# A spectral filter and a two-layer product in one kernel: where the halves of the second product, the splits of the weights and the first load of w_out stand

## The chip, the cores and the metric

The kernel runs on one core of a Trainium2 chip. The metric is the time on the device in microseconds (us). In what follows PE is the matrix engine (TensorE), PEld its weight loads, DVE is VectorE, ACT is ScalarE, POOL is GpSimd and SP is SyncE, which here only issues DMAs.

## The reference

Two parts follow each other. A spectral filter works along the sequence of 3008 positions, for 8 batches of 256 features, and its result goes through two matrix products with a leaky ReLU between them.

```python
X = np.fft.rfft(x, axis=1)                       # x: (8, 3008, 256)
Yr = Xr @ w_r - Xi @ w_i + b_r                   # w_r, w_i: (256, 256)
Yi = Xr @ w_i + Xi @ w_r + b_i
Yr, Yi = soft_threshold(Yr, 0.01), soft_threshold(Yi, 0.01)
y = np.fft.irfft(Yr + 1j * Yi, n=3008, axis=1)   # then reshaped to (24064, 256)
h = y @ w_in                                     # w_in: (256, 2048), as 64-bit floats
g = np.maximum(0.01 * h, h)
out = g @ w_out                                  # w_out: (2048, 256), as 64-bit floats
```

## The kernel before

**The spectral part.** 3008 is 47 x 64, so each Fourier transform is done as two smaller ones by matrix products, per batch `b`. `fwd(b)` makes the transform of length 47 (lines 219 to 322) and stores it in DRAM as `u_dram`. `mid(b)` (lines 325 to 461) reads it back in twelve pieces as tiles `u`, makes the transform of length 64 (`stage_b`, line 358), splits the result into a high and a low part, the tiles `eh` and `el` (lines 366 to 375), applies w_r and w_i (`proj`), thresholds (lines 405 to 407, tile `t`, in the list `thresholded`), multiplies by signs (lines 411 and 415), splits into `zh` and `zl` (lines 420 to 424), transforms back (`stage_g`) and stores `v_dram`. `inverse` makes the last transform from tiles `vin` read back from `v_dram`. For batch 0 `fwd` and `mid` run ahead of everything else, in plain 32-bit matmuls; they are the start. For the batches 1 to 7 they are generators that are woven into the two products, and they use high and low parts of the weights, which `split_consts` makes (lines 108 to 113: one ACT copy at line 112 and one DVE subtraction at line 113 for each of six tiles).

**The two products.** Every number is a high and a low part, and each product of two blocks is three matmuls: high by high, high by low, low by high. Tokens come in 47 chunks of 512, `ci`; the 2048 middle columns in eight pieces, `q`. This gives 376 steps. In a step the first product is done by seven block products instead of eight (a Strassen-Winograd scheme). `moe_a` (line 549) makes four of them, in two PSUM banks `b1` and `b2` of 2 x 256 columns: 12 matmuls at line 92. ACT then copies one quarter to `p1` (line 559), and DVE adds: `u2` (line 560), and the fourth quarter of the tile `g`, which the profile calls `gf` (lines 562 and 563). `moe_b` (line 566) adds the other three block products to the same banks: 9 matmuls at line 92. They overwrite what lines 559 to 563 read, so they wait for them. Then come ACT at line 573, DVE at line 574, ACT at line 576 (the leaky ReLU), ACT's copy `gh` (line 578, high part) and DVE's subtraction `gl` (line 580, low part). `moe_o` (line 583) makes the second product of a step in two halves, `eh` 0 and 1, of 6 matmuls of 512 columns each, at line 593. It runs `LAG` = 2 steps behind, so it reads `gh` and `gl` of two steps ago.

**What sets the order.** On each engine the instructions run in a fixed order. A scheduler sorts them when the program is built, by a simulated timeline of its own. `in_order` (line 84) binds the matmuls of `moe_a`, `moe_b` and `moe_o` to each other in the order in which `moe` (line 624) issues them; the other instructions the scheduler places around them. `tc.issue_after(x)` keeps an instruction behind `x` in that order.

**The loads of w_out.** `load_wout` (line 175) reads it in eight pieces of 512 KB into tiles `raw`. The first two take the buffers of `gl`, which are free in the start.

Of the kernel before, what the change touches and what calls it, by code (L numbers as in the profile page):

```python
# [18 lines left out]
N1, N2, NK1 = 47, 64, 24  # L19
# [11 lines left out]
def spectral_mlp_kernel(  # L31
# [35 lines left out]
    sync, act, dve, pool = nc.sync, nc.scalar, nc.vector, nc.gpsimd  # L67
# [16 lines left out]
    def in_order(part, *args):  # L84

        with tc.issue_after(mlp[0].ins) if mlp else nullcontext():
            part(*args)
# [87 lines left out]
    def load_wout():  # L175

        n = CS // D
        ov = w_out.bitcast(U32).rearrange("(a p) f -> p a f", p=P)
        raws = []

        def load(early):
            k = len(raws)
            tag, bufs = ("gl", 2) if early else (("e", 1), ("z", 1))[k % 2]
            raw = sb.tile([P, CS, 2], U32, name="raw", tag=tag, bufs=bufs)
            with tc.issue_after(zeroed[0].ins):
                pool.dma_start(raw.rearrange("p (a f) w -> p a (f w)", a=n), ov[:, k * n:(k + 1) * n, :])
            raws.append(raw)

        for k in range(2):
            load(True)  # L190
        yield 1
        consts["wout"] = tuple(
            sb.tile([P, NF, D], F32R, name=f"wout_{p}", tag=f"wout_{p}", bufs=1) for p in ("hi", "lo"))
        for c in range(NF // n):
            a = sb.tile([P, CS], F32, name="cva", tag="zf", bufs=1)
            q = sb.tile([P, CS], F32, name="cvq", tag="u", bufs=3)
            float64_parts(raws[c], a, q)
            dh, dl = (w[:, c * n:(c + 1) * n, :] for w in consts["wout"])
            a, q = (t.rearrange("p (a f) -> p a f", a=n) for t in (a, q))
            act.copy(dh, a)  # L200
            dve.tensor_sub(a, a, dh.bitcast(F32))
            converted.append(dve.tensor_add(dl, a, q))
            yield 1
            while c >= 1 and len(raws) < min(c + 3, NF // n):
                load(False)
# [2 lines left out]
    u_dram = {}  # L208
    v_dram = {}

    reads, written, turned, turning, thresholded, zeroed = [], [], [], [], [], []
    NX = -(-NS // 2)

    XW = [(0, 2), (2, 6), (6, 10), (10, 13)]
# [110 lines left out]
    def mid(b):  # L325
# [51 lines left out]
        def proj(j):  # L377

            e = e_t.pop(j)
            ps_k = bank("psf", 2) if b else bank("pso", 2)  # L380
            ps_y = None if b else bank("psf", 2)

            for dst, c, w in ((0, 2, "wr"), (0, 1, "wn"), (D, 0, "wd")):
                if c == 1 and b:
                    ps_y = bank("psf", 2)
                products((ps_k if c == 2 else ps_y)[:, dst:dst + D], [
                    (tuple(t[:, a, c, :] for t in e), tuple(t[:, a, :] for t in consts[w]) if b else (consts[w + "32"][0][:, a, :],)) for a in range(NH)
                ] + ([((ones,), (bz[:, D if c == 0 else 0:][:, :D],))] if b == 0 and c < 2 else []))
                if c == 2:
                    kc = sb.tile([P, D], F32, name="kc", tag="kc")  # L390
                    act.copy(kc, ps_k[:, :D])  # L391
                if c == 2 and b:
                    kb = sb.tile([P, 2, D], F32, name="kb", tag="kb", bufs=1)
                    pool.tensor_add(kb, bias, kc.unsqueeze(1).broadcast_to([P, 2, D]))  # L394
                if c:
                    yield 6 * D
                if c == 2 and b and j:
                    stage_g(j - 1)
                    yield 3 * CS
            t = sb.tile([P, 2, D], F32, name="t", tag="t" if b else "v", bufs=1 if b else 2)  # L400
            c = sb.tile([P, 2, D], F32, name="c", tag="kb", bufs=1)
            if b == 0:
                dve.tensor_add(t, ps_y.rearrange("p (r d) -> p r d", r=2), kc.unsqueeze(1).broadcast_to([P, 2, D]))
            else:
                dve.tensor_add(flat(t), ps_y, flat(kb))
            dve.tensor_scalar(c, t, LAMBDA, -LAMBDA, ALU.min, ALU.max)
            thresholded.append(dve.tensor_sub(t, t, c))
            zf = z0[j % 3] if b == 0 else sb.tile([P, 2, D], F32, name="zf", tag="zf", bufs=1)
            for i in range(2):
                s = slice(64 * i, 64 * (i + 1))  # L410
                act.copy(zf[:64, i, :], t[s, 0, :])  # L411
                if b == 0 and j == NPAIR - 1:
                    dve.tensor_scalar(zf[64:, i, :], t[s, 1, :], sign[s, NK1 + j:NK1 + j + 1], None, ALU.mult)
                else:
                    act.mul(zf[64:, i, :], t[s, 1, :], sign[s, NK1 + j:NK1 + j + 1])  # L415
            if b == 0:
                z_t[j] = (zf,)
                yield 6 * D
                return
            z = sb.tile([P, 2, 2, D], F32R, name="zh", tag="z", bufs=1)  # L420
            zh, zl = z[:, 0], z[:, 1]
            act.copy(zh, zf)
            dve.tensor_sub(zl, zf, zh.bitcast(F32))
            z_t[j] = (zh, zl)
            yield 6 * D
# [198 lines left out]
    def moe():  # L624

        for i, (ci, q) in enumerate(steps):
            if q == 0:
                nxt = tokens(ci + 1) if ci + 1 < nch else iter(())
            in_order(moe_a, ci, q)
            if i >= LAG:  # L630
                in_order(moe_o, *steps[i - LAG], 0)
            next(nxt, None)
            yield ci + (q + 0.5) / NQ
            in_order(moe_b, ci, q)
            if i >= LAG:
                in_order(moe_o, *steps[i - LAG], 1)
            next(nxt, None)
            if q == NQ - 1:
                for _ in nxt:
                    pass  # L640
            yield ci + (q + 1) / NQ
        for s in steps[-LAG:]:
            for eh in range(NH):
                in_order(moe_o, *s, eh)
# [34 lines left out]
    sign = const.tile([P, NK1 + NPAIR], F32, name="sign")  # L679
# [14 lines left out]
    with tc.issue_after(turned[0].ins):  # L694
        act.copy(bz[:1], brow[:1])
        act.copy(bz[32:33], brow[32:33])
        act.mul(fa32[:, 2], fa32[:, 1], -1.0)
        split_consts()
    dve.tensor_sub(bz[32:33], brow[32:33], bz[32:33].bitcast(F32))
    m0 = Stream(mid(0), MID)  # L700
    m0.to(0.001)
# [12 lines left out]
    for i in range(1, 17):  # L714
        m0.to(i / 16)
        if i in (1, 5, 8):
            load_win(1 + i // 4, (sync, sync), reads[-1])
        if i in (5, 10):
            convert_win(i // 5)
        if 5 <= i < 12:  # L720
            next(fp.gen)
        if i == 13:
            next(wout)
        if i >= 14:

            if i < 16:
                next(fp.gen)
# [144 lines left out]
```

## Time and profile before

| | |
|---|---|
| median of 3 runs | 2892.94 us (2890.22 to 2896.18) |
| profiled execution | 2892.13 us, its span 2890.3 us |
| busy share of the span | PE 93%, PEld 80%, DVE 65%, ACT 58%, POOL 9% |
| mean granted clock of PE | 0.985 |

The start ends at about 130 us, when the first matmul of the products runs. From there to about 2400 us the products run beside the spectral part of the other batches, and then nearly alone. Rows of a timeline read: start, duration, engine, line, operation, what it writes and reads, and in brackets how long the engine was idle before it and what ended that. Rows of waits read: who waited for whom, us in total, how often, the longest. A matmul's listed duration is longer than the distance to the next one, since matmuls overlap; distances between starts tell what PE gets done.

### The profile page before, as it was taken

Reading aid. Unit: us, or ns where it says so; the run is one execution under the profiler, and the core shown is the slowest. Engines: PE = TensorE matmul, PEld = TensorE weight load, DVE = VectorE, ACT = ScalarE, POOL = GpSimd, SP = SyncE. Lnnn points to the kernel's source line nnn. Section 1 sums busy time; section 2 is a strip of 40 time slices with the busy share of each in tenths; the row PEclk is TensorE's granted clock in tenths of the full one; section 3 lists DMA queues with packets and bytes.
Section 4 is the critical chain, followed back from the end, with each engine's and each line's share of the span. In section 5 each row is a group of like instructions: output and inputs, shape, how many; then the busy total and the mean of one; then the engine's idle time right before and its main releaser. Section 6 shows DMA issues by size and latency. Waiting matters only on the chain.

```text
span 2890.3 us, 43048 instructions
## 1 busy us (share of the span) xinstructions
PE 2673.7 (93%) x16300; PEld 2307.6 (80%) x16300; DVE 1892.0 (65%) x3403; ACT 1671.0 (58%) x3174; POOL 248.9 (9%) x188
## 2 busy tenths in 40 slices
PE   6799999999999999999999999999999999999988
PEld 4578878888788887888878887788887888777777
DVE  5787766666666666676666666666666766555554
ACT  4667655656566654666546565566555665454443
POOL 0001120001200011000110001100011000000000
PEclk9999999999999999999999999999999999999999
DMA  9422132111321112121221112211122111000000
GB/s 253 141 79 55 44 94 59 42 48 30 98 63 46 37 50 76 55 58 33 62 79 51 42 35 61 82 57 40 33 67 81 55 44 33 25 25 15 15 8 15
DMA packets 117416, 165.16 MB, mean 57 GB/s; under 512 B 13437, under 2 KB 69401, under 8 KB 117209
## 3 DMA queue, kind: packets, MB, share of 16 engines
q1 hardware_dynamic: 79473, 115.02, 13.1%
q10 hardware_dynamic: 36584, 43.20, 5.9%
q0 software_dynamic: 1152, 4.19, 0.5%
q8 instruction: 128, 2.10, 0.3%
q14 instruction: 79, 0.65, 0.1%
HBM read 86.60 MB, written 75.76 MB: 56 GB/s over the span
## 4 chain that ended last, share of the span: by engine, by line
PE 46%; DVE 27%; ACT 18%; issue 4%; DMA 3%; POOL 1%; SPq 0%; DVEq 0%; ACTq 0%; POOLq 0%
PE psh L92 18%; PE pso L593 16%; PE psf L78 7%; DVE gl L580 7%; ACT gh L578 6%; ACT gf L576 5%; DVE gf L574 4%; DVE gf L562 3%; DVE u L560 2%; DVE gf L563 2%; PE psf L496 2%; PE psf L358 2%; ACT zf L415 2%; DVE yl L523 1%; ACT zf L411 1%
## 5 line engine op out<-in xcount | busy, mean ns | idle before, releaser
L92 PE MATMUL psh<-yh,win_hi 128*128 128x256 f32 x2632 | 791.7, 301 | 113.9 <-DVE gf L563 78.3
L580 DVE TENSOR_TENSOR gl<-gf,gh 128x1024 fp32r<-128x1024 f32 x376 | 465.2, 1237 | 441.6 <-ACT gh L578 434.2
L92 PE MATMUL psh<-yl,win_hi 128*128 128x256 f32 x2632 | 741.1, 282 | 0.0
L92 PE MATMUL psh<-yh,win_lo 128*128 128x256 f32 x2632 | 739.4, 281 | 0.0
L92 PEld LDWEIGHTS psh<-yh,win_hi 128*128 128x128 f32 x2632 | 499.5, 190 | 235.1 <-DVE gf L563 122.9
L593 PE MATMUL pso<-gh,wout_hi 128*128 128x512 f32 x1504 | 597.4, 397 | 0.0
L593 PE MATMUL pso<-gh,wout_lo 128*128 128x512 f32 x1504 | 597.1, 397 | 0.0
L593 PE MATMUL pso<-gl,wout_hi 128*128 128x512 f32 x1504 | 594.5, 395 | 0.0
L576 ACT ACTIVATE gf<-gf 128x768 f32<-128x768 f32 x376 | 318.2, 846 | 437.0 <-DVE gf L574 427.1
L92 PEld LDWEIGHTS psh<-yl,win_hi 128*128 128x128 f32 x2632 | 500.4, 190 | 23.6 <-issue 0.6
L92 PEld LDWEIGHTS psh<-yh,win_lo 128*128 128x128 f32 x2632 | 499.3, 190 | 0.3 <-issue 0.2
L578 ACT CAST gh<-gf 128x1024 fp32r<-128x1024 f32 x376 | 395.1, 1051 | 10.3 <-PE pso L593 4.0
L574 DVE TENSOR_TENSOR gf<-psh,u 128x512 f32<-128x512 f32 x376 | 258.4, 687 | 199.7 <-PE psh L92 199.2
L593 PEld LDWEIGHTS pso<-gl,wout_hi 128*128 128x128 f32 x1504 | 285.9, 190 | 65.4
L593 PEld LDWEIGHTS pso<-gh,wout_hi 128*128 128x128 f32 x1504 | 286.0, 190 | 35.0
L593 PEld LDWEIGHTS pso<-gh,wout_lo 128*128 128x128 f32 x1504 | 286.0, 190 | 31.8
L573 ACT ACTIVATE gf<-psh 128x256 f32<-128x256 f32 x376 | 145.3, 386 | 258.6 <-PE psh L92 238.8
L394 POOL TENSOR_TENSOR kb<-bias,kc 128x512 f32<-128x512 f32 x84 | 127.1, 1513 | 1616.0 <-ACT kc L391 1507.9
L560 DVE TENSOR_TENSOR u<-psh,p 128x256 f32<-128x256 f32 x376 | 157.1, 418 | 90.5 <-ACT p L559 90.4
L562 DVE TENSOR_TENSOR gf<-psh,u 128x256 f32<-128x256 f32 x376 | 158.7, 422 | 28.2
L563 DVE TENSOR_TENSOR gf<-psh,gf 128x256 f32<-128x256 f32 x376 | 157.8, 420 | 6.1
L559 ACT COPY p<-psh 128x256 f32<-128x256 f32 x376 | 137.2, 365 | 14.9 <-PE psh L92 13.0
(135 smaller groups left out, 3271.8 us busy)
## 6 DMA issues: line engine op xcount, KB each, us to landing
u<-u_dram SPq DMA_DIRECT2D x192, 128.0 KB, 2.7
out_dram<-ob SPq DMA_DIRECT2D x94, 256.0 KB, 2.0
vin<-v_dram SPq DMA_DIRECT2D x96, 240.0 KB, 3.3
v_dram<-v ACTq DMA_DIRECT2D x168, 128.0 KB, 2.4
xin<-x_dram SPq DMA_DIRECT2D x85, 240.0 KB, 3.0
u_dram<-xin ACTq DMA_DIRECT2D x72, 240.0 KB, 2.4
raw<-w_out_dram POOLq DMA_DIRECT2D x8, 512.0 KB, 5.0
win_raw<-w_in_dram SPq DMA_DIRECT2D x8, 512.0 KB, 7.6
```

The costliest lines, as they stand in the source:

```text
L78: last = nc.tensor.matmul(dst, a, b, start=(i == 0), stop=(i == len(terms) - 1))
L92: mlp[:] = [nc.tensor.matmul(dst, a, b, start=start and i == 0, stop=i == 2, skip_group_check=True)]
L559: act.copy(p1, b1[:, lo])
L560: dve.tensor_add(u2, b1[:, hi], p1)
L562: dve.tensor_add(g[:, 3], b2[:, hi], u2)
L563: dve.tensor_add(g[:, 3], b2[:, lo], g[:, 3])
L573: act.activation(g[:, 0], b1[:, lo], AF.Prelu, alpha=SLOPE)
L574: dve.tensor_add(g[:, 1:3], b2.rearrange("p (k n) -> p k n", k=2), u2.unsqueeze(1).broadcast_to([P, 2, HT]))
L576: act.activation(g[:, 1:4], g[:, 1:4], AF.Prelu, alpha=SLOPE)
L578: cp = act.copy(gh, g)
L580: parted[:] = [cp, dve.tensor_sub(gl, g, gh.bitcast(F32))]
L593: mlp[:] = [nc.tensor.matmul(po, a[:, f, s], r[:, i], start=(f == 0 and j == 0), stop=(f == NF - 1 and j == 2),)]
```

## The change

Four things change.

In `moe`, both halves of the second product now stand between `moe_a` and `moe_b`. Before, the second half stood behind `moe_b`.

`split_consts` is called in turn 4 of the loop over `mid(0)`, behind the latest threshold and the latest sign multiplication issued by then, which a new list `signed` records. Before, it was called ahead of `mid(0)`.

The first two loads of w_out are issued by SP, behind the last load of `u` for batch 0 (`reads[-1]`). Before, POOL issued them behind its first memset.

The later loads of w_out stay on POOL as they were.

```diff
-            with tc.issue_after(zeroed[0].ins):
-                pool.dma_start(raw.rearrange("p (a f) w -> p a (f w)", a=n), ov[:, k * n:(k + 1) * n, :])
+            with tc.issue_after(reads[-1].ins if early else zeroed[0].ins):
+                (sync if early else pool).dma_start(raw.rearrange("p (a f) w -> p a (f w)", a=n), ov[:, k * n:(k + 1) * n, :])
...
-                    act.mul(zf[64:, i, :], t[s, 1, :], sign[s, NK1 + j:NK1 + j + 1])
+                    signed[:] = [act.mul(zf[64:, i, :], t[s, 1, :], sign[s, NK1 + j:NK1 + j + 1])]
...
             yield ci + (q + 0.5) / NQ
-            in_order(moe_b, ci, q)
             if i >= LAG:
                 in_order(moe_o, *steps[i - LAG], 1)
+            in_order(moe_b, ci, q)
...
         act.mul(fa32[:, 2], fa32[:, 1], -1.0)
-        split_consts()
...
+        if i == 4:
+            with tc.issue_after(thresholded[-1].ins), tc.issue_after(signed[-1].ins):
+                split_consts()
```

How this moves instructions is shown at three places. First PE, at one step of the last stage. `psh` are the banks `b1` and `b2`, `pso` the sums of the second product, one for each half; the numbers tell tiles apart. Before:

```order
L593 MATMUL pso_27365<-gl_27571,wout_hi_886 128x512
L92 MATMUL psh_27628<-yh_27027,win_hi_169 128x256
L92 MATMUL psh_27628<-yl_27028,win_hi_169 128x256
L92 MATMUL psh_27628<-yh_27027,win_lo_170 128x256
L92 MATMUL psh_27629<-yh_27027,win_hi_169 128x256
L92 MATMUL psh_27629<-yl_27028,win_hi_169 128x256
L92 MATMUL psh_27629<-yh_27027,win_lo_170 128x256
L92 MATMUL psh_27629<-yh_27027,win_hi_169 128x256
L92 MATMUL psh_27629<-yl_27028,win_hi_169 128x256
L92 MATMUL psh_27629<-yh_27027,win_lo_170 128x256
L593 MATMUL pso_27388<-gh_27569,wout_hi_886 128x512
```

And PE at the same step of the changed kernel:

```order
L593 MATMUL pso_27365<-gl_27577,wout_hi_886 128x512
L593 MATMUL pso_27372<-gh_27575,wout_hi_886 128x512
L593 MATMUL pso_27372<-gh_27575,wout_lo_887 128x512
L593 MATMUL pso_27372<-gl_27577,wout_hi_886 128x512
L593 MATMUL pso_27372<-gh_27575,wout_hi_886 128x512
L593 MATMUL pso_27372<-gh_27575,wout_lo_887 128x512
L593 MATMUL pso_27372<-gl_27577,wout_hi_886 128x512
L92 MATMUL psh_27628<-yh_27027,win_hi_169 128x256
```

The nine matmuls of `moe_b` stood between the halves; now the second half (`pso_27372`) follows the first, and `moe_b` follows it.

Second DVE, in the same stage. Before, from line 574 of one step to that of the next:

```order
L574 TENSOR_TENSOR gf_25211<-psh_25194,u2_25208 128x512
L580 TENSOR_TENSOR gl_25246<-gf_25211,gh_25244 128x1024
L560 TENSOR_TENSOR u2_25275<-psh_25260,p1_25274 128x256
L562 TENSOR_TENSOR gf_25278<-psh_25261,u2_25275 128x256
L563 TENSOR_TENSOR gf_25278<-psh_25261,gf_25278 128x256
L574 TENSOR_TENSOR gf_25278<-psh_25261,u2_25275 128x512
```

And DVE between the same two instructions of the changed kernel:

```order
L574 TENSOR_TENSOR gf_25211<-psh_25194,u2_25208 128x512
L560 TENSOR_TENSOR u2_25275<-psh_25260,p1_25274 128x256
L562 TENSOR_TENSOR gf_25278<-psh_25261,u2_25275 128x256
L563 TENSOR_TENSOR gf_25278<-psh_25261,gf_25278 128x256
L580 TENSOR_TENSOR gl_25252<-gf_25211,gh_25250 128x1024
L574 TENSOR_TENSOR gf_25278<-psh_25261,u2_25275 128x512
```

The subtraction `gl` of a step stood ahead of the next step's lines 560 to 563, and now stands behind them. On ACT, in the same way, line 559 of the next step has moved from behind lines 576 and 578 to ahead of them.

Third PE, in the middle of the program, at a projection of batch 2: line 358 transforms a tile `u`, and line 78 with `wr` and `eh` is the first matmul that reads what is made of the result. Before:

```order
L358 MATMUL psf_4449<-fb_94,u_4174 128x2x64 x4
L92 MATMUL psh_4323<-yh_3794,win_hi_169 128x256
L92 MATMUL psh_4323<-yl_3795,win_hi_169 128x256
L92 MATMUL psh_4323<-yh_3794,win_lo_170 128x256
L78 MATMUL psf_4488<-wr_hi_177,eh_4454 128x256
```

And PE in front of the same projection (`eh_4454`) in the changed kernel; its transform stands 43 rows ahead of it:

```order
L593 MATMUL pso_4276<-gh_4610,wout_hi_886 128x512
L593 MATMUL pso_4276<-gh_4610,wout_lo_887 128x512
L593 MATMUL pso_4276<-gl_4612,wout_hi_886 128x512
L593 MATMUL pso_4276<-gh_4610,wout_hi_886 128x512
L593 MATMUL pso_4276<-gh_4610,wout_lo_887 128x512
L593 MATMUL pso_4276<-gl_4612,wout_hi_886 128x512
L78 MATMUL psf_4488<-wr_hi_339,eh_4454 128x256
```

A whole second product and a `moe_a` now stand between the transform and the projection, where three matmuls did.

More of the change, by code (lines that the diff above doesn't have):

```diff
@@ L209, in spectral_mlp_kernel @@
     v_dram = {}
-    reads, written, turned, turning, thresholded, zeroed = [], [], [], [], [], []
+    reads, written, turned, turning, thresholded, zeroed, signed = [], [], [], [], [], [], []
     NX = -(-NS // 2)
```

## The prediction

> **What bounds the kernel now.** I read the page's busy shares first, then the three stages as windows, then who TensorE (PE) waited for in each stage, then one period of the last stage in order of time.
>
> ```profile
> PE 2673.7 (93%) x16300; PEld 2307.6 (80%) x16300; DVE 1892.0 (65%) x3403; ACT 1671.0 (58%) x3174; POOL 248.9 (9%) x188
> ...
> L92 PE MATMUL psh<-yh,win_hi 128*128 128x256 f32 x2632 | 791.7, 301 | 113.9 <-DVE gf L563 78.3
> L580 DVE TENSOR_TENSOR gl<-gf,gh 128x1024 fp32r<-128x1024 f32 x376 | 465.2, 1237 | 441.6 <-ACT gh L578 434.2
> ```
>
> PE is the bound: 93% busy, and most of its idle time stands before line 92, the seven block products of the first matrix product, waiting for a VectorE (DVE) addition. The next two views, the windows and the waits of PE alone, give start (0 to 200 us), middle (spectral work beside the two products, 200 to 2400) and end (the products nearly alone).
>
> ```profile
> 0.00:200.00 200.00, 152.97 (x703) 113.43 (x704) 140.78 (x258) 119.23 (x228) 8.04 (x15) 0.91 0.58 166
> 200.00:2400.00 2200.00, 2075.85 (x13009) 1824.00 (x13008) 1481.29 (x2673) 1318.16 (x2540) 239.55 (x172) 0.99 0.20 56
> 2400.00:2890.30 490.30, 444.90 (x2592) 370.21 (x2590) 269.96 (x474) 233.62 (x407) 1.29 (x1) 0.99 0.06 19
> ```
>
> Columns: length, busy time of PE, weight loads, DVE, ACT, POOL, then granted clock. In the end stage DVE works 55% and ACT 48% of the time, and PE still idles 45 us: a latency, not a throughput. Waits of PE, first the middle stage, then the end:
>
> ```profile
> PE psh L92 <- DVE gf L563: 46.1, 92, 2.0
> PE psh L92 <- DVE u L560: 20.4, 61, 1.1
> PE psf L78 <- ACT eh L373: 16.2, 9, 2.8
> PE psf L78 <- DVE xz L266: 11.6, 24, 1.8
> PE psf L78 <- DVE xz L267: 6.0, 16, 0.5
> PE psf L78 <- ACT zh L422: 5.0, 6, 2.0
> PE psf L78 <- DVE yc L529: 4.1, 2, 2.1
> ```
> ```profile
> PE psh L92 <- DVE gf L563: 26.6, 64, 1.7
> PE psh L92 <- DVE u L560: 10.4, 55, 0.5
> ```
>
> One period of the end stage:
>
> ```profile
> 2702.30 0.38 PE L92 MATMUL psh<-yh,win_hi 128*128 128x256 f32 x1 [0.17 <-DVE u L560]
> ...
> 2702.64 0.28 PE L92 MATMUL psh<-yh,win_lo 128*128 128x256 f32 x1
> 2702.81 0.42 DVE L563 TENSOR_TENSOR gf<-psh,gf 128x256 f32<-128x256 f32 x1
> ...
> 2703.29 0.39 PE L92 MATMUL psh<-yh,win_hi 128*128 128x256 f32 x1 [0.37 <-DVE gf L563]
> 2703.51 0.28 PE L92 MATMUL psh<-yl,win_hi 128*128 128x256 f32 x1
> ...
> 2704.10 0.40 PE L593 MATMUL pso<-gh,wout_hi 128*128 128x512 f32 x1
> 2704.30 0.69 DVE L574 TENSOR_TENSOR gf<-psh,u 128x512 f32<-128x512 f32 x1 [1.07 <-PE psh L92]
> ...
> 2705.03 0.85 ACT L576 ACTIVATE gf<-gf 128x768 f32<-128x768 f32 x1 [1.69 <-DVE gf L574]
> ...
> 2705.49 0.28 PE L92 MATMUL psh<-yh,win_hi 128*128 128x256 f32 x1
> ...
> 2705.91 1.05 ACT L578 CAST gh<-gf 128x1024 fp32r<-128x1024 f32 x1
> ...
> 2706.89 0.40 PE L593 MATMUL pso<-gh,wout_hi 128*128 128x512 f32 x1
> 2706.99 1.23 DVE L580 TENSOR_TENSOR gl<-gf,gh 128x1024 fp32r<-128x1024 f32 x1 [1.99 <-ACT gh L578]
> ...
> 2708.13 0.42 DVE L560 TENSOR_TENSOR u<-psh,p 128x256 f32<-128x256 f32 x1
> ...
> 2708.60 0.39 PE L92 MATMUL psh<-yh,win_hi 128*128 128x256 f32 x1 [0.17 <-DVE u L560]
> ```
>
> The reader is to see a loop. `moe_b` of a step ends at 2704.10; then L574 (0.69), L576 (0.85), L578 (1.05) and `gl` L580 (1.23) run one behind the other, and only behind `gl` does DVE come to L560, L562 and L563 of the next step, for which that step's `moe_b` waits. The period is 2708.60 - 2702.30 = 6.30 us. PE's own work in it: 12 matmuls of `moe_a` from 2705.49 to 2706.89, 1.40; two halves of six matmuls, each 2705.49 - 2704.10 = 1.39; nine matmuls of `moe_b` at 1.40/12 = 0.117, 1.05; in all 5.23. So 1.07 us a step is lost.
>
> **The change, part by part.** *Both halves of `moe_o` ahead of `moe_b`.* Between `moe_a`'s end and `moe_b`'s start PE now has 2.78 us of work instead of 1.39. The order shows that DVE and ACT were re-sorted too: L560, L562, L563 of a step now stand ahead of the `gl` before it. From `moe_b`'s end to the next `moe_b`'s second product PE has 1.40 + 2.78 + 0.35 = 4.53 us; the DVE chain there is 0.69 + 3 x 0.42 = 1.95 us plus passing times. 2.5 us of room is more than all waits seen in the end stage, so there I let them vanish. What a wait costs: at a spacing of 0.117 the matmul of 2703.29 would have stood at 2702.76, so it lost 0.53 where 0.37 is listed, and its successor came 0.22 behind it instead of 0.117: 0.26 on top of the listed idle time. End stage: 26.6 + 10.4 + 119 x 0.26 = 68 us. The ceiling is every step of the stage at 1.07:
>
> ```profile
> L560 DVE TENSOR_TENSOR u<-psh,p x73: 415/417/426, 2404.0 to 2877.1; 128x256 f32<-128x256 f32 x73
> ```
>
> 73 x 1.07 = 78 us. I take 68.
>
> Middle stage, the same two waits: 46.1 + 20.4 + 153 x 0.26 = 106 us. Here DVE also serves the spectral streams. It is busy 1481 us, of which some 295 steps take 1.24 + 0.69 + 3 x 0.42 = 3.19 us each, 941; the rest is 540, 1.8 us a step, against 2.5 us of room. On average it fits, but it comes in lumps, and all of a lump can stand ahead of L563. I take four fifths, 85 us; the ends are half (53) and all (106).
>
> What the wider lead costs: `gl` of a step is read by `moe_o` two steps later, and that lead shrinks by one half, 1.39 us: from 3 x 1.39 + 2 x 1.40 + 1.05 + two matmuls, 0.46 = 8.5 us to 7.1. The chain L574 to `gl` takes 0.69 + 0.85 + 1.05 + 1.23 = 3.8 us, a little over 4 with the passing times. Cost nothing; cover 3 us. `gh` and `gl` have two buffers, and are now free before they are rewritten, since their readers moved ahead.
>
> *The spectral streams, re-sorted by it.* In the middle a projection could stand right behind its input:
>
> ```profile
> 473.93 0.39 PE L78 MATMUL psf<-wr_hi,eh 128*128 128x256 f32 x1 [2.48 <-ACT eh L373]
> ```
>
> Before it stood only three matmuls behind the transform that feeds it (13 of 84 projections stand like that in the order); now the nearest has 18 rows between. So the waits for eh go: 16.2, with yc (which stands at the same place) 4.1, and 11 x 0.26, together 23 us. xz and zh, 22.6 + 46 x 0.26 = 35 us, are also spaced wider but keep short chains: half, 17 us. Sum 40; ends 10 (places change, waits stay) and 58.
>
> *The clock.* It was 0.99 in both stages, 1% of 2690 us, some 27 us lost, and as long waits go I give back 16; the ends are 0 and 27. [...]
>
> *Weights split in the middle stage of the start; w_out's first words by SP.* Before, ACT held six splits ahead of the first transform, and POOL sent 1 MB of w_out into the writes of u_dram:
>
> ```profile
> 37.74 0.62 ACT L112 CAST wn_hi<-w 128x512 fp32r<-128x512 f32 x1
> ...
> 38.38 3.60 PE L358 MATMUL psh<-fb,u 128*128 128x128 f32 x16 [14.82 <-ACT wn_hi L112]
> ```
> ```profile
> 108.03 0.70 ACT L131 ACTIVATE cvq<-raw 128x512 f32<-128x512 uint32 x1 [2.53 <-DMA raw<-w_out_dram]
> ```
> ```profile
> 0.00:50.00 50.00, 24.98 (x90) 16.32 (x91) 18.31 (x34) 17.41 (x32) 2.09 (x7) 0.86 0.88 252
> 50.00:100.00 50.00, 48.15 (x231) 37.27 (x230) 43.61 (x76) 44.38 (x87) 0.30 (x1) 1.00 0.73 200
> ```
>
> 1 MB at the 252 GB/s of the first 50 us (last column) is 4.2 us; this the first transform can gain if the u loads are what it waits for, nothing if not. Against it: the six splits, three at 0.62 and three of at most half that, 2.8 us of ACT and about as much of DVE, now fall where ACT is busy 44.4 of 50 us and PE 48.2, and the two w_out loads come late on SP, behind the last u loads, two issues that the stores of v behind them on SP wait for. If they land after ACT reaches them, ACT's queue stands as it did at 108.03, 2.53 us each. [...] From -4.2 to +2.8 + 5.1 = +7.9; I take 0, since the two sides are alike. POOL's queue only gets shorter.
>
> *The end.* Behind the last `moe_b` PE had 18 matmuls to cover the last chain, now 12: 1.39 us less, +1 us.
>
> Sum: 68 + 85 + 40 + 16 - 0 - 1 = 208. The profiled execution took 2892.1 us (span 2890.3 and 1.8 around it), 0.8 below the median of 2892.9. 2892.1 - 208 = 2684 us. A change under 0.2%, about 6 us, could not be told from none.
>
> **The rivals.** *The waits move inside the middle stage.* For it: DVE and ACT are fixed queues, and a shorter PE time raises their load from 67% to about 72% (1481 of 2200 - 141); against it, the room worked out above. Then the middle gives half, 53, the streams 10, the clock 5, the end stage still 68, less 1: 135, so 2757 us.
> *All of it goes.* 78 + 106 + 58 + 27 = 269, the start 4, less 1: 2620 us. Against it speak the lumps.
> *`moe_o` becomes the waiter (slower).* If in the middle other work stretches the chain from L574 to `gl` beyond the 7.1 us lead, PE waits at line 593 instead. That happens from 3 us of foreign work per step between them on ACT and DVE; to eat the gain it must exceed the lead by 208/295 = 0.71 us in every step of the stage, so a chain of 7.8 us decides. At 1 us over it is 2684 + 295 = 2979 us. The 1.8 us of stream work a step on DVE and a like share on ACT speak against it.
> *The clock stays as it is.* Should its dips come from something else than the long waits, the 16 us are not given back: 2684 + 16 = 2700 us. [...]
> *The change does nothing.* The order might be restored by the scheduler; the order of the built program shows that it is not. Left at two in a hundred.
>
> **How the numbers follow.** Forecast, around 2684: 0.5; clock as it is, around 2700: 0.12; both within 2655 to 2720. Waits move, 2720 to 2780: 0.2. Nearly all goes, 2600 to 2655: 0.13. Slower: 0.03; unchanged 0.02. To hold eight in ten the range takes the forecast, the upper part of "all goes" and the nearer half of "moved": 2638 to 2750. Faster 0.95, same 0.02, slower 0.03.
>
> **What would show it.** In the end stage the period of L560 falls to 5.23 us and the waits of line 92 for L563 and L560 vanish (right), or line 593 gets waits for `gl` (wrong). In the middle the waits of line 92 fall from 66 us below 20, those for eh from 16 to near none; if they stay, DVE's queue order was mis-read. In the start, PE's first line-358 matmul comes before 38.4 us and the first product no later than now; an ACT wait for raw near 85 us would show the w_out term. Wrong I would be by a middle stage whose DVE lumps are larger than 2.5 us in most steps.

## The result, and the profile after

The changed kernel takes 2612.97 us (2611.39 to 2616.30, 4 runs) against 2892.86 us (4 runs on the same chip): a ratio of 0.9033, 95% interval 0.9018 to 0.9049, so 280 us less. The forecast was 2684 us with a range down to 2638; the time lies 25 us under that range, nearest to the rival "all of it goes" at 2620. The profiled execution took 2616.3 us, its span 2614.5.

The same groups of the page as before, and line 593, which the prediction named as a possible waiter:

```profile
PE 2544.1 (97%) x16300; PEld 2284.3 (87%) x16300; DVE 1896.2 (73%) x3403; ACT 1667.9 (64%) x3174; POOL 234.9 (9%) x186
...
L92 PE MATMUL psh<-yh,win_hi 128*128 128x256 f32 x2632 | 753.0, 286 | 16.3 <-DVE gf L563 12.3
...
L593 PE MATMUL pso<-gl,wout_hi 128*128 128x512 f32 x1504 | 591.0, 393 | 0.5 <-DVE gl L580 0.5
...
L580 DVE TENSOR_TENSOR gl<-gf,gh 128x1024 fp32r<-128x1024 f32 x376 | 470.3, 1251 | 91.2 <-ACT gh L578 88.6
```

PE is busy for 97% of the span instead of 93%. The idle time of line 92 fell from 113.9 to 16.3 us, and line 593 has one wait of 0.5 us. DVE's idle time ahead of `gl` fell from 441.6 to 91.2 us: `gl` comes later in DVE's queue now, when `gh` is nearly there. The stages (length, PE, weight loads, DVE, ACT, POOL, granted clock); the middle stage now ends near 2200 us, so the windows are cut there:

```profile
0.00:200.00 200.00, 155.56 (x706) 114.41 (x707) 139.06 (x256) 117.60 (x226) 5.31 (x12) 0.92 0.57 165
200.00:2200.00 2000.00, 1978.64 (x12973) 1800.02 (x12973) 1480.64 (x2670) 1312.42 (x2531) 225.68 (x171) 1.00 0.22 61
2200.00:2614.50 414.50, 409.86 (x2625) 369.87 (x2623) 276.47 (x479) 237.85 (x418) 3.88 (x3) 1.00 0.07 24
```

In the middle stage PE idles 21 us instead of 124, in the end stage 5 instead of 45. All waits of PE of some size in the middle stage, and then in the end stage:

```profile
PE psf L358 <- DMA u<-u_dram: 9.6, 6, 2.6
PE psh L92 <- DVE gf L563: 6.5, 6, 2.8
PE psh L92 <- DVE u L560: 2.5, 3, 1.9
PE psf L78 <- ACT eh L373: 1.8, 3, 1.1
```
```profile
PE pso L593 <- DVE gl L580: 0.5, 1, 0.5
PE psh L92 <- DVE gf L563: 0.3, 1, 0.3
```

The waits for `xz`, `zh` and `yc` are gone altogether. The largest that is left, 9.6 us, was 1.5 us before: at the first transform of each of six batches PE now arrives before the loads of `u`.

One period of the end stage, DVE first, then ACT:

```profile
2562.29 0.69 DVE L574 TENSOR_TENSOR gf<-psh,u 128x512 f32<-128x512 f32 x1 [1.07 <-PE psh L92]
2563.40 0.42 DVE L560 TENSOR_TENSOR u<-psh,p 128x256 f32<-128x256 f32 x1 [0.41 <-ACT p L559]
2563.93 0.42 DVE L562 TENSOR_TENSOR gf<-psh,u 128x256 f32<-128x256 f32 x1
2564.39 0.42 DVE L563 TENSOR_TENSOR gf<-psh,gf 128x256 f32<-128x256 f32 x1
2565.22 1.23 DVE L580 TENSOR_TENSOR gl<-gf,gh 128x1024 fp32r<-128x1024 f32 x1 [0.41 <-ACT gh L578]
2567.52 0.69 DVE L574 TENSOR_TENSOR gf<-psh,u 128x512 f32<-128x512 f32 x1 [1.07 <-PE psh L92]
```
```profile
2562.99 0.38 ACT L559 COPY p<-psh 128x256 f32<-128x256 f32 x1 [1.01 <-PE psh L92]
2563.26 0.85 ACT L576 ACTIVATE gf<-gf 128x768 f32<-128x768 f32 x1
2564.14 1.05 ACT L578 CAST gh<-gf 128x1024 fp32r<-128x1024 f32 x1
```

The reader is to see three things. The period is 2567.52 - 2562.29 = 5.23 us, PE's own work as the prediction summed it. `gl` stands behind L563, no longer between L574 and L560. And on ACT the copy `p` (L559) stands ahead of L576 and of the `gh` cast: the short chain that PE waits for goes first on both engines.

Where the time went, by the start of single steps (first matmul of the step, us):

| | before | after | gained here | predicted here |
|---|---|---|---|---|
| step 0 | 126.2 | 127.8 | -1.6 | 0 |
| step 303 | 2401.2 | 2196.9 | 205.9 | 85 + 40 + 16 = 141 |
| step 375 | 2874.4 | 2598.7 | 71.4 | 68 |
| end of span | 2890.3 | 2614.5 | 0.1 | -1 |

The end stage came out as forecast. The stretch from step 0 to step 303 gave 65 us more.

### The profile page after: what moved, and what is told of

Same layout as the page of the kernel before. It is cut to its first block, busy times and chain, and to the rows that moved or that the text cites. A ratio compares the mean times of both kernels' runs of the same rounds, so it can differ in the third digit from the quotient of the medians.

```text
span 2614.5 us, 42635 instructions
## 1 busy us (share of the span) xinstructions
PE 2544.1 (97%) x16300; PEld 2284.3 (87%) x16300; DVE 1896.2 (73%) x3403; ACT 1667.9 (64%) x3174; POOL 234.9 (9%) x186
## 4 chain that ended last, share of the span: by engine, by line
PE 89%; DVE 4%; DMA 3%; ACT 3%; issue 1%; SPq 0%; ACTq 0%; DVEq 0%
PE pso L593 37%; PE psh L92 34%; PE psf L78 11%; PE psf L496 3%; PE psf L358 3%; PE psh L78 1%; DMA u<-u_dram 1%; DMA u_dram<-xin 1%; DVE yl L523 1%; DMA win_raw<-w_in_dram 0%; DMA v_dram<-v 0%; DVE gl L580 0%; ACT zf L415 0%; DVE gf L574 0%; DMA raw<-w_out_dram 0%
## 5 line engine op out<-in xcount | busy, mean ns | idle before, releaser
L92 PE MATMUL psh<-yh,win_hi 128*128 128x256 f32 x2632 | 753.0, 286 | 16.3 <-DVE gf L563 12.3
L593 PE MATMUL pso<-gh,wout_lo 128*128 128x512 f32 x1504 | 590.3, 392 | 0.0
L580 DVE TENSOR_TENSOR gl<-gf,gh 128x1024 fp32r<-128x1024 f32 x376 | 470.3, 1251 | 91.2 <-ACT gh L578 88.6
L574 DVE TENSOR_TENSOR gf<-psh,u 128x512 f32<-128x512 f32 x376 | 259.1, 689 | 251.8 <-PE psh L92 250.7
L578 ACT CAST gh<-gf 128x1024 fp32r<-128x1024 f32 x376 | 396.4, 1054 | 7.4 <-ACT p L559 0.2
L576 ACT ACTIVATE gf<-gf 128x768 f32<-128x768 f32 x376 | 320.0, 851 | 54.0 <-DVE gf L574 52.3
L559 ACT COPY p<-psh 128x256 f32<-128x256 f32 x376 | 140.0, 372 | 212.7 <-PE psh L92 211.7
L394 POOL TENSOR_TENSOR kb<-bias,kc 128x512 f32<-128x512 f32 x84 | 119.1, 1418 | 1461.1 <-ACT kc L391 1375.6
L560 DVE TENSOR_TENSOR u<-psh,p 128x256 f32<-128x256 f32 x376 | 158.6, 422 | 112.5 <-ACT p L559 110.3
L562 DVE TENSOR_TENSOR gf<-psh,u 128x256 f32<-128x256 f32 x376 | 159.2, 423 | 30.1 <-PE psh L92 1.8
L563 DVE TENSOR_TENSOR gf<-psh,gf 128x256 f32<-128x256 f32 x376 | 159.0, 423 | 9.0
```

Of the source, the lines that this page charges most:

```text
L92: mlp[:] = [nc.tensor.matmul(dst, a, b, start=start and i == 0, stop=i == 2, skip_group_check=True)]
L559: act.copy(p1, b1[:, lo])
L560: dve.tensor_add(u2, b1[:, hi], p1)
L562: dve.tensor_add(g[:, 3], b2[:, hi], u2)
L563: dve.tensor_add(g[:, 3], b2[:, lo], g[:, 3])
L574: dve.tensor_add(g[:, 1:3], b2.rearrange("p (k n) -> p k n", k=2), u2.unsqueeze(1).broadcast_to([P, 2, HT]))
```

## The experiments

In the tables and sums below, the "loss" of a matmul is the distance from the start before it to its own start, less the median of that distance for predecessors of the same source line and the same shape. It is worked out from the starts of all matmuls and counts waits too short for the rows of waits. The middle stage is there steps 20 to 303, the end stage steps 304 to 374.

### e1 and e2: the moved half alone, and the start's edits alone

e1 is the kernel before with this alone, e2 the changed kernel with this undone:

```diff
-            in_order(moe_b, ci, q)
             if i >= LAG:
                 in_order(moe_o, *steps[i - LAG], 1)
+            in_order(moe_b, ci, q)
```

> The kernel before with the second half of moe_o ahead of moe_b, and none of the start's edits. Theory A (all of the 280 us comes from the moved half): 2613 us, within 4, and the first line-358 matmul at 38.4 us as before. Theory B (the earlier first transform, 33.3 instead of 38.4 us, carries some of it): 2617 to 2620 us. If the moved half had given only the 208 us of the forecast and the start the rest: 2680 us.

> The kernel after with moe_o's second half back behind moe_b: the start's edits alone. Theory A: no change, 2893 us within 2, because the first product's steps begin no earlier than before (step 0 at 127.8 against 126.2 us) although the first transform comes 5 us earlier. Theory B: 2888 us.

Measured: e1 2609.46 us (2608.49 to 2613.51), ratio 0.9021 [0.9008, 0.9033]; e2 2890.93 us (2886.94 to 2892.27), ratio 0.9991 [0.9982, 0.9999], against 2892.50 for the kernel before in the same runs. Theory A holds: the moved half is the whole gain. e1's first transform came at 35.98 us, not at the 38.4 that was expected; the next two runs bear on that. The start's edits alone are worth 1.6 us by these medians, so next to nothing of an earlier first transform is left at the end.

### e3 and e4: the start's edits, one by one

e3 is the changed kernel with the splits back ahead of `mid(0)`, e4 the changed kernel with the first loads of w_out back on POOL:

```diff
e3:
         act.mul(fa32[:, 2], fa32[:, 1], -1.0)
+        split_consts()
...
-        if i == 4:
-            with tc.issue_after(thresholded[-1].ins), tc.issue_after(signed[-1].ins):
-                split_consts()
e4:
-            with tc.issue_after(reads[-1].ins if early else zeroed[0].ins):
-                (sync if early else pool).dma_start(raw.rearrange("p (a f) w -> p a (f w)", a=n), ov[:, k * n:(k + 1) * n, :])
+            with tc.issue_after(zeroed[0].ins):
+                pool.dma_start(raw.rearrange("p (a f) w -> p a (f w)", a=n), ov[:, k * n:(k + 1) * n, :])
```

> The kernel after with the weight splits back ahead of the first transform, and w_out's first words still by SP. Theory S (the splits in the middle of the start hold ACT near 59 us, and the two waits of line 78 for zf, 1.1 and 1.8 us long at 58 and 78 us, are what gives the 5 us back): the first transform stays at 33.3, because ACT stands idle before it, the first product begins 3 to 5 us earlier, 2608 to 2610 us. Theory N (the lead is lost whatever ACT does, since the loads or PE's own work bound the start): within 1.5 us of after, 2613.

> The kernel after with w_out's first two loads issued by POOL again, as before; the splits stay in the middle of the start. If w_out's 1 MB in the writes of u_dram was what held the first transform: first line-358 matmul near 38 us instead of 33.3, and, by theory S, the splits still cost their share, 2616 to 2618 us. If the loads had no part: first transform 33.3 and 2613 us.

Measured: e3 2610.83 us (2608.43 to 2614.66), ratio 0.9024 [0.9011, 0.9036], e4 2619.85 us (2617.75 to 2620.77), ratio 0.9053 [0.9040, 0.9065]. In the changed kernel the first transform and the two waits for line 415's `zf` are these rows:

```profile
33.31 0.98 PE L358 MATMUL psh<-fb,u 128*128 128x128 f32 x3 [10.54 <-DMA u<-u_dram]
...
58.47 1.13 PE L78 MATMUL psh<-zf,w 128*128 128x512 f32 x2 [2.62 <-ACT zf L415]
...
77.80 1.82 PE L78 MATMUL psh<-zf,w 128*128 128x512 f32 x2 [2.02 <-ACT zf L415]
```

The first transform stood at 38.38 before and stands at 33.31 now, waiting for `u` itself. These waits are 2.62 and 2.02 us; e3's expectation took the durations, 1.13 and 1.82, for them. Over all traces of this document, nine with POOL's loads have the first transform between 35.66 (e4) and 38.38 us, median 37.30, and seven with SP's between 32.43 (e3) and 34.44, median 33.35. So w_out's 1 MB ahead of the loads of `u` costs the first transform about 4 us, near the 4.2 of the prediction's bound; e4 lies at the early end of its group, 2.3 us before the 38 that was expected, and its time is 2 us above the expected range.

The lead doesn't last to the products. Step 0 begins between 123.4 and 126.2 us in the eight traces with the start of before, and between 124.5 and 127.8 in the five with the changed start. It is not shown that the waits for `zf` take the lead: e3, which has the splits early, still has 4.6 us of them ahead of 130 us, with line 411's, against 6.9 in the changed kernel and 3.1 before. With the moved half in all four, the times are:

| first loads of w_out by | splits ahead of `mid(0)` | splits in the middle of the start |
|---|---|---|
| POOL | 2609.46 (e1) | 2619.85 (e4) |
| SP | 2610.83 (e3) | 2612.97 (after) |

With POOL's loads the kernel with the splits' new place is 10 us slower, but not by what theory S says: in the traces of e1 and e4, step 20 begins at 278.2 and 279.0 us, and step 303 at 2190.0 and 2200.8. The 10 us arise in the middle stage, where the scheduler put `gl` ahead of line 560 in 9 steps of e4 instead of 5, and where the loss is 41.7 us instead of 32.4. With SP's loads the difference is 2 us, within the spread, although step 0 begins at 121.8 us in e3 and 127.8 in the changed kernel, so theory S and theory N are not told apart there. SP's loads gain 7 us where the splits stand late and nothing where they stand early. No combination beats e1, which has none of the start's edits.

### e5, e6 and e13: the queue of DVE against the order on PE

The forecast explained the gain by PE's work between `moe_a` and `moe_b`. The rival theory is that only the place of `gl` in DVE's queue matters, which the scheduler changed when PE's order changed. e5 keeps PE's old order and holds `gl` back:

```diff
-        dve.tensor_add(g[:, 3], b2[:, lo], g[:, 3])
+        added = dve.tensor_add(g[:, 3], b2[:, lo], g[:, 3])
...
+        if late:                  # the moe_b of the step before
+            low_part(added)
...
-        parted[:] = [cp, dve.tensor_sub(gl, g, gh.bitcast(F32))]
+        with tc.issue_after(behind.ins) if behind is not None else nullcontext():
+            parted[:] = [cp, dve.tensor_sub(gl, g, gh.bitcast(F32))]
```

e6 keeps the changed kernel's order on PE, and e13 the old one, and both hold the next step back, as the loop before did:

```diff
-        act.copy(p1, b1[:, lo])
-        dve.tensor_add(u2, b1[:, hi], p1)
+        with tc.issue_after(parted[0].ins) if parted else nullcontext():
+            act.copy(p1, b1[:, lo])
+        with tc.issue_after(parted[1].ins) if parted else nullcontext():
+            dve.tensor_add(u2, b1[:, hi], p1)
```

> The kernel before with its old order on PE (one half of moe_o on either side of moe_b), but DVE takes gl of a step only behind L563 of the next step, in all 375 steps (before: gl first in 251 of them). Between the end of moe_b and the second product of the next moe_b PE has the same 4.53 us in both orders. Theory Q (the place of gl in DVE's queue made the loop): period 5.23 us in the end stage, and most of the 280 us, 2610 to 2650 us. Theory P (it takes 2.78 us of PE work between moe_a and moe_b): period still near 6.3, 2870 to 2893 us.

> The kernel after with its new order on PE, but L559 and L560 of a step held behind gh and gl of the step before on ACT and DVE, as in the loop before. Theory Q: the loop is back, period near 6.3 us in the end stage and at least that in the middle, 2850 to 2930 us. Theory P: period 5.23, 2613 us.

> The kernel before, old order on PE, with L559 and L560 held behind gh and gl in all 375 steps (before: 251). If the loop through gl alone sets the time, whatever PE's order: 3026 us, as with the new PE order and the same held queues. If the new PE order is itself a loss with the old queues: 2930 to 2970, the 118 other steps then losing about half a microsecond more each, as the 166 did.

Measured: e5 2695.92 us (2693.02 to 2696.10), ratio 0.9325 [0.9311, 0.9339]; e6 3025.77 us (3015.13 to 3030.05), ratio 1.0463 [1.0442, 1.0484]; e13 3019.99 us (3015.22 to 3020.59), ratio 1.0446 [1.0432, 1.0460].

Theory Q holds and P falls. With `gl` first on DVE (and `p` behind `gh` on ACT), the time is 3020 and 3026 us whatever PE's order; with `gl` last and PE's old order 195 us of the 280 are there. The old order still misses e5's range by 46 us, which e15 takes up. e6 was slower than expected, since its queues are worse than those before, where `gl` came first in 251 of 375 steps only. DVE in the end stage of e13 (its lines 576, 582, 562, 564, 565 are the 574, 580, 560, 562, 563 of before):

```profile
2950.68 0.69 DVE L576 TENSOR_TENSOR gf<-psh,u 128x512 f32<-128x512 f32 x1 [1.08 <-PE psh L92]
2953.37 1.23 DVE L582 TENSOR_TENSOR gl<-gf,gh 128x1024 fp32r<-128x1024 f32 x1 [2.00 <-ACT gh L580]
2954.51 0.42 DVE L562 TENSOR_TENSOR u<-psh,p 128x256 f32<-128x256 f32 x1
2955.03 0.42 DVE L564 TENSOR_TENSOR gf<-psh,u 128x256 f32<-128x256 f32 x1
2955.49 0.42 DVE L565 TENSOR_TENSOR gf<-psh,gf 128x256 f32<-128x256 f32 x1
2957.00 0.69 DVE L576 TENSOR_TENSOR gf<-psh,u 128x512 f32<-128x512 f32 x1 [1.08 <-PE psh L92]
```

DVE idles 2.00 us because the head of its queue, `gl`, waits for `gh`, and the three additions that PE needs stand behind it. The period is 6.32 us, that of before, and in e6, with 2.78 us of PE work between `moe_a` and `moe_b`, the median is 6.30.

The traces of before and after, with the steps from 20 on sorted by the queue order that DVE executed (loss per step in us, of `moe_b`'s nine matmuls and of the whole step):

| queue order, stage | before: steps, `moe_b`, whole | after: steps, `moe_b`, whole |
|---|---|---|
| `gl` ahead of L560, middle | 166, 0.54, 0.89 | 5, 1.45, 1.89 |
| `gl` between L560 and L562, middle | 11, 0.55, 2.77 | 3, 0.07, 0.57 |
| `gl` between L562 and L563, middle | 90, 0.30, 0.37 | 46, 0.13, 0.44 |
| `gl` behind L563, middle | 17, 0.24, 0.39 | 230, 0.01, 0.01 |
| `gl` ahead of L560, end | 64, 1.01, 1.15 | 0 |
| `gl` between L562 and L563, end | 7, 0.72, 0.71 | 2, 0.01, 0.02 |
| `gl` behind L563, end | 0 | 69, 0.01, 0.01 |

e12's expectation gives these losses from a reckoning that pools the 256-column and 512-column matmuls of line 78; that adds about 0.17 us to the whole loss of a middle step, so its 0.18 is 0.01 here, its 39 us are 31, and its 228 and 56 steps are 230 and 54.

### e8 and e9: how much room is left

e8 puts one more DVE addition (zeros onto themselves) into every step, e9 two:

```diff
+        for _ in range(1 if summed else 0):          # e9: 2
+            with tc.issue_after(summed[0].ins):      # behind the last L574
+                dve.tensor_add(extra, extra, extra)  # 128x512
         dve.tensor_add(u2, b1[:, hi], p1)
```

> The kernel after with one more DVE addition of 128x512 (a tile of zeros onto itself, about 0.65 us) between L574 and the next L560 in every step: it measures how much of PE's room is left. Theory R (2.5 us of room against 1.8 us of stream work a step on average, and lumps seldom larger): at most 10 us slower than after, period in the end stage still 5.23. Theory L (the lumps of stream work only just fit): waits of line 92 for L563 return in the middle stage, 40 us or more slower than after.

> As the last one with two such additions, about 1.3 us, which brings DVE from 5.05 to some 6.35 us of the 6.83 us that a step of the middle stage takes. Theory R: the room of 2.5 us is overdrawn by 0.6 us in the middle stage on average, 10 to 60 us slower than after; the end stage still at 5.23. Theory L: 100 us or more slower.

Measured: e8 2672.57 us (2672.07 to 2674.67), ratio 0.9246 [0.9231, 0.9261], 60 us above after; e9 2757.88 us (2756.35 to 2759.26), ratio 0.9542 [0.9527, 0.9556], 145 above. That is theory L by the number. But the additions also made the scheduler sort `gl` forward again. In e8 176 middle steps keep it behind L563 and lose 0.02 us in `moe_b`, 0.04 in all, against 0.01 and 0.01 without the addition; 83 have it between L562 and L563 (0.18 and 0.39), and 25 ahead of both (1.2 and more in all). These 108 steps hold 74 of the 82 us that e8's middle stage loses. As a measure of the room these two runs failed, since they changed the queue order along with the load.

### e12, e14 and e11: the queue order held, and the room once more

e12 is e1 with e5's edit, so the new order on PE and `gl` behind L563 in every step. e14 adds the loads of w_out by SP. e11 is e12 with two more additions pinned in front of L560:

```diff
+                x = dve.tensor_add(extra, extra, extra)   # the second of two
+        with tc.issue_after(x.ins) if summed else nullcontext():
+            dve.tensor_add(u2, b1[:, hi], p1)
```

> New order on PE and gl held behind L563 of the next step on DVE in every step, with the old start. In the trace of after the 228 middle steps with that queue order lose 0.18 us each, and the 56 with another order 39 us together (most of it in 44 steps in which gl stands between L562 and L563). Theory Q (the queue order is what is left to gain): 2592 to 2602 us against the 2609 of the moved half alone. If those 39 us come from the stream work that stands there, whatever the order: 2609, within 3.

> As the last one, with w_out's first words by SP and the splits where they were before. If the 2.5 to 3 us that the first transform comes earlier lasts to the end: 3 us faster than the last one; if it is lost in the start, as in the kernel after: the same within 2 us.

> The held order of e12 with two more DVE additions of 128x512 (0.68 us each) pinned ahead of L560 in every step: the room once more, with the queue order now fixed. DVE then works 6.4 of the 6.8 us of a middle step. Theory R (a room of 2.5 us that the streams' 1.8 us use on average): overdrawn by 0.7 us in an average step of the middle stage, 100 to 200 us slower than e12; end period 5.23. Theory W (what cost the time in e8 and e9 was gl's changed place, the room is wider since stream work on PE widens it too): at most 40 us slower than e12.

Measured: e12 2595.26 us (2593.84 to 2596.30), ratio 0.8979 [0.8966, 0.8991]; e14 2600.28 us (2599.38 to 2603.54), ratio 0.8999 [0.8987, 0.9012]; e11 2669.54 us (2666.62 to 2670.97), ratio 0.9236 [0.9223, 0.9248].

e12 is where theory Q put it, 17.7 us faster than the changed kernel and 14 faster than e1, from which it differs by the held order alone; it has the lowest median of all. The loss of the middle stage fell from e1's 32.4 us to 20.8, so not all of what the steps with another order lost came back. Its page and its waits in the window from 200 to 2200 us:

```profile
PE 2538.4 (98%) x16300; PEld 2284.6 (88%) x16300; DVE 1899.3 (73%) x3403; ACT 1665.9 (64%) x3174; POOL 234.0 (9%) x188
...
L92 PE MATMUL psh<-yh,win_hi 128*128 128x256 f32 x2632 | 748.7, 285 | 9.2 <-DVE gf L563 8.1
```
```profile
PE psh L92 <- DVE gf L563: 4.1, 2, 3.5
PE psf L78 <- ACT eh L373: 1.9, 2, 1.6
PE psh L92 <- DVE yl L523: 1.6, 3, 0.7
PE psf L358 <- DMA u<-u_dram: 0.6, 1, 0.6
```

The waits for the loads of `u` went too, which I had not expected of a change in DVE's queue. e14 missed both expectations: its first transform comes at 34.44 instead of 37.42, yet step 0 is 1.3, step 4 is 4.9, step 20 is 3.0 and step 303 is 5.0 us later than in e12. With e2 to e4 that makes the start's edits worth nothing or a small loss here; where the time is lost stays open.

e11 lies between its two theories, 74 us above e12. DVE is busy 91% of the middle stage there:

```profile
200.00:2200.00 2000.00, 1960.76 (x12709) 1769.99 (x12709) 1821.89 (x3192) 1292.70 (x2472) 246.03 (x169) 1.00 0.21 60
```

`moe_b` loses 0.14 us a step in the middle stage instead of 0.03, the whole step 0.24 instead of 0.07; in the end stage 0.13 and 0.14 instead of 0.01. So 1.36 us of foreign DVE work in every step costs about 0.2 us of it (74 us over 376 steps): most of it fits beside the stream work as long as `gl` is not ahead of the three additions. Two additions cost 145 us in e9 and 74 here, so about half of e9's price was the load and the rest, as far as additions that are pinned at different places compare, the queue order.

### e15 and e16: the place of `p` in ACT's queue

With `gl` held back, the old order on PE still took 2696 us and the new one 2595. In e5 a second queue shows why:

```profile
2640.47 0.85 ACT L578 ACTIVATE gf<-gf 128x768 f32<-128x768 f32 x1 [1.60 <-DVE gf L576]
2641.35 1.05 ACT L580 CAST gh<-gf 128x1024 fp32r<-128x1024 f32 x1
2642.30 0.36 ACT L559 COPY p<-psh 128x256 f32<-128x256 f32 x1
```
```profile
2642.70 0.43 DVE L560 TENSOR_TENSOR u<-psh,p 128x256 f32<-128x256 f32 x1 [2.26 <-ACT p L559]
```

Here `p` stands behind the `gh` cast (L578 of before) on ACT, and DVE idles 2.26 us for it; e5's period is 5.43 us. e15 is e5 with the cast held behind `p`, e16 is e12 with `p` held behind the cast:

```diff
e15:
-        act.copy(p1, b1[:, lo])
+        copied = act.copy(p1, b1[:, lo])
+        if late:                  # the moe_b of the step before
+            high_part(copied)
...
+        with tc.issue_after(behind.ins) if behind is not None else nullcontext():
+            late[:] = [(ci, q, gh, g, act.copy(gh, g))]
e16:
-        act.copy(p1, b1[:, lo])
+        with tc.issue_after(late[0][4].ins) if late else nullcontext():   # gh of the step before
+            act.copy(p1, b1[:, lo])
```

> e5 (old order on PE, gl held behind L563 of the next step on DVE), and now also the gh cast held behind L559 of the next step on ACT, in all 375 steps (e5: L559 behind gh in 192). Theory A (the 100 us between e5 and e12 come from L559 behind gh: the chain L574, L576, L578, L559, L560, L562, L563 closes a loop of 5.43 us): period 5.23 in the end stage, 2595 to 2640 us. Theory C (they come from the work that PE has between moe_a and moe_b, 1.39 against 2.78 us): 2690 to 2700 us, as e5.

> e12 (new order on PE, gl held behind L563 of the next step), and L559 held behind the gh cast of the step before in all steps (e12: in 5). Theory A: the period goes to 5.4 us in the end stage, and the time to 2690 to 2740 us in spite of the new order on PE. Theory C: 2595 to 2610 us.

Measured: e15 2635.47 us (2632.74 to 2636.89), ratio 0.9114 [0.9101, 0.9128], median period of the end stage 5.23 us; e16 2820.43 us (2812.69 to 2823.56), ratio 0.9759 [0.9742, 0.9775], median period 5.43 us. Theory A holds for e15 in both numbers, for e16 in the period; its time is 80 us beyond the range I gave. Its waits in the window from 200 to 2200 us (L561 and L564 are L560 and L563 of before):

```profile
PE psh L92 <- DVE u L561: 42.0, 43, 2.8
PE psh L92 <- DVE gf L564: 30.6, 43, 1.8
```

`moe_b` loses 0.42 us a step in the middle stage there, against 0.03 in e12. Stream work on ACT delays the cast, and with it `p`: in 86 middle steps ACT does at least 1 us of other work between the end of `moe_b` and the next `p`, and the next `moe_b` waits 0.74 us on average; in 139 it does none, and the wait is 0.05.

All with one scale, in us:

| order on PE | queues as the scheduler made them | `gl` first, `p` behind `gh` | `gl` last, `p` behind `gh` in all steps or half | `gl` last, `p` ahead of `gh` |
|---|---|---|---|---|
| old | 2892 | 3020 (e13) | 2696 (e5, 192 steps) | 2635 (e15) |
| new | 2609 (e1) | 3026 (e6) | 2820 (e16, all steps) | 2595 (e12) |

With the same two queues, the order on PE moves the time by 6 us (second column) or 40 (last); with the same order on PE, the two queues move it by 385 and 431. The third column holds different numbers of steps in its two rows, so its 2696 and 2820 don't compare the orders on PE. The change did not need the second half of `moe_o` between `moe_a` and `moe_b` for the larger part of its gain: the old order with both queues mended gains 256 of the 280 us.

## Why the prediction was right or wrong

*The loop of the end stage: right.* L574, L576, L578, `gl`, L560, L562, L563 was the chain; the period went from 6.30 to 5.23 us and the stage gave 71.4 us where 68 were taken. e13 shows the same loop under force.

*What breaks it: the step that failed.* The prediction said that both halves of `moe_o` ahead of `moe_b` make the room, 4.53 us, and named DVE's new order beside it. But the work from `moe_b`'s end to the next `moe_b`'s second product is one `moe_a`, two halves and three matmuls in the old order as well: 4.53 us in both. That number could not be what changed. The new place of `gl` and of `p` was (e5, e15). e6 shows PE's new order without it: 3026 us, no better than the 3020 of the old order with the same queues (e13), and both some 130 us slower than before. What did grow is the work between `moe_a` and `moe_b`, from 1.39 to 2.78 us; it is worth 40 us with `gl` last and `p` ahead of `gh` (e15 against e12) and nothing with `gl` first.

*The middle stage's four fifths, 85 us: too small, for that reason.* The discount was for lumps of stream work that fill the room. In after, the loss of `moe_b` over the middle steps fell from 126.6 to 15.8 us, so 111 were gained, about the 106 that I took for all of it. e11 puts 1.36 us more on DVE in each step and loses 0.11 of it in `moe_b`. The lumps were the wrong fear; the 54 middle steps of after whose `gl` still stands ahead of L563 have 13 of the 16 us that are left.

*The streams, 40 us, and the clock, 16: too small.* What the middle steps lose outside `moe_b` fell from 92 to 18 us, by 74, where these two terms have 56, and the rows of waits for `eh`, `xz`, `zh` and `yc` went from 43 to 1.8 us. Taking half of `xz` and `zh` was wrong: between one `xz`'s last use and the next one's first PE now has at least ten matmuls, 1.96 us at the median spacings, instead of three, 0.35 us, and none of their waits is left.
Of 15 stretches of 3.41 us at half clock between 200 us and the end 3 are left, at about 1.5 us each (last section), so 12 x 1.5 = 18 us came back and not 16.

Of the 65 us that the middle gave beyond the forecast, `moe_b` has 26 and the rest of the middle steps 18. Another 10 were gained between step 0 and step 20, and some 11 these losses don't place.

*The start, 0, and the end, -1: right* within 2 us. Both sides of the start are there, a lead of 5 us at the first transform and nothing of it at step 0, but what takes the lead back is not shown. The late w_out loads that the prediction priced at up to 5.1 us did not hold ACT near 85 us in the changed kernel; in e3 ACT waited 1.55 us for one at 83.18.

*The rivals.* "All of it goes" had every term at its ceiling and missed by 7 us: 78 for the end stage's 71, 106 for `moe_b`'s 111, 85 for the 74 of the streams and the clock. It was close term by term, but it had the same account of the room. "`moe_o` becomes the waiter" did not come: one wait of 0.5 us. "The clock stays as it is" did not come either: its mean went from 0.985 to 0.992. The prediction reckoned with a queue that waits at one DMA load of the start, by the 2.53 us of the row at 108.03, and did not put the gain down to the places of `gl` and `p`, where DVE idled 2.00 us (e13, ahead of `gl`) and 2.26 us (e5, for `p` behind the cast).

## What to carry to other kernels

Where an engine waits for a short chain on another engine, read what stands ahead of that chain in the other engine's queue, and what that in turn waits for; here two instructions that nobody needed soon, a subtraction of 1.23 us and a cast of 1.05 us, stood ahead of three additions of 0.42 us each that the bound engine was waiting for. When a changed order on one engine comes with a re-sorted order on others, test the two apart before you credit the first, and hold the order that gains by an explicit dependency: the scheduler's own choice left 14 us here (e1 against e12). A room or a slack explains a gain only if it differs between the two versions, so work it out for both.

## What the runs showed of the hardware

Between 200 us and the last matmul the granted clock of PE was 1.00 in both traces, except in single or double stretches of 3.41 us at 0.50. The windows below are from the changed kernel, around the first transform of a batch (columns as above, the granted clock is the third number from the right):

```profile
457.00:460.40 3.40, 1.47 (x13) 1.30 (x12) 0.30 (x1) 0.39 (x1) 0.00 (x0) 1.00 0.44 129
460.40:463.80 3.40, 3.40 (x19) 3.40 (x17) 1.92 (x5) 1.53 (x4) 0.00 (x0) 0.50 0.34 103
463.80:467.20 3.40, 3.40 (x21) 2.99 (x21) 2.82 (x7) 2.64 (x6) 0.00 (x0) 1.00 0.00 0
```

PE was busy 1.47 us of the first stretch, with one wait of 1.93 us in it, and ran at half clock for the whole next stretch of 3.41 us, in which it was busy throughout. Behind 200 us, line 92's matmuls start 0.213 us apart (median) in the stretches at half clock of either trace and 0.117 us apart outside them. From these two spacings I estimate that a stretch at half clock costs 3.41 x (1 - 0.117/0.213) = 1.5 us.

In the trace of before, 15 such stretches lie between 200 us and the last matmul, each behind one in which PE was busy between 0.92 and 2.07 of 3.41 us. Counted on the same grid of 3.41 us in that trace, every one of the 13 stretches with less than 1.78 us of busy PE was followed by half clock, of 11 with 1.79 to 2.07 us two were, and none with more. The wait of 1.93 us above was followed by a stretch that cost some 1.5 us more, by the estimate. The counts show what stood ahead of the stretches at half clock, not what causes them.

In the middle stage of before the matmuls lost more than the listed waits: the seven rows of waits that the prediction shows of it hold 109 us, the starts of its matmuls a loss of 219 us over the steps from 20 to 303, of which the stretches at half clock account for some 20, by the same estimate (13 of 1.5 us).
